# Second and last product of an attention, MoE, MoE kernel: T1's product goes ahead of T2's, and each sum is made in the step of its own product

## The chip, the cores and the metric

The kernel runs on one core of one Trainium2 chip. The metric is device time of one launch in microseconds (us). Three runs of the kernel before gave 1398.18, 1399.5 and 1400.55, median 1399.5.

## The reference

The input goes through three parts. The first is an attention over 32 memory slots per head (8 batches, 8 heads, 576 positions, 64 wide); its output, taken as rows of 512, has 4608 of them. Then come two feed-forward blocks, one after the other, each with its own weights of 512 x 2048 and 2048 x 512:

```python
def _moe_ref(x, w_in, w_out):          # x is 4608 x 512
    h = x @ w_in
    r = np.maximum(h, 0.0)
    g = r * r
    return (g @ w_out).astype(np.float32)

def _moe2_ref(x, w_in, w_out):
    h = x @ w_in
    g = h * (1.0 / (1.0 + np.exp(-h)))
    return (g @ w_out).astype(np.float32)

def reference(**kwargs):
    attn_out = _attn_ref(**attn_kwargs)
    x = np.ascontiguousarray(attn_out.transpose(0, 2, 1, 3)).reshape(B * S, H * D)
    x = _moe_ref(x=x, **moe_kwargs)
    return _moe2_ref(x=x, **moe2_kwargs)
```

## The kernel before

Four large products follow one another on TensorE (PE). The first (L635, first block of rows L612) joins the attention with `w_in` of the first feed-forward block. The **second product** is g1 times the first `w_out`, the third product (L940) is its result times the second `w_in`, and the **last product** is g2 times the second `w_out`. The second and the last are made by the same function, `second` (L735), with PE's matmuls on L821. The change touches these two alone.

The three later products use a scheme with seven products of half-size matrices in place of eight. The moving matrix of a block of 768 rows is cut in four quarters B11, B21, B12 and B22 (a quarter is half of the inner dimension by 384 rows, for all of that half's eight slices of 128). From them four sums are made: T1 = B12 - B11, T2 = B22 - T1, T3 = B22 - B12 and T4 = B21 - T2. The seven products take B11, B21, T2, T1, T3, B22 and T4 (`PRODUCTS`, L698), numbered n = 0 to 6, each with its own combination of the weights, which lies in slot n of the weight tiles W[q] (`slot`, L685; product 6 shares slot 1 with product 1, and `next_w`, L691, loads one in place of the other). There are eight weight tiles, q = 0 to 7, one for each pair of the inner dimension's slices.

Every factor is split in a part that the matmul takes exactly (`hi`, made by a cast on ScalarE, ACT, L792) and the rest (`lo`, a subtraction on VectorE, DVE, L793); the text calls them cast and split. Three matmuls of 128 x 128 by 384 columns stand for one product of such pairs.

**Steps.** `second` runs over `(b, n, h)`: six blocks b of 768 rows, seven products n, four quarters h of the inner dimension (two slices each). One step has 12 matmuls of 384 columns: 2 slices, 2 halves of the output, 3 pairings. The step's moving tile c has six buffers, and `combos` (L770), which makes the sums, the cast and the split for one step, is called four steps ahead of the step's matmuls (`AHEAD`, `ahead`). The sums are made in place: T1 over B11 (L780), T3 over B12 (L786), T4 over B21 (L789); T2 has a tile of its own (L784). Before the change T1's sum and T2's are both made in the steps of T2, T3's in the steps of T1, T4's in the steps of T3. In the second product the quarters are squared on ACT first (L768), B11 and B21 in the steps of n = 0, B12 and B22 in those of n = 1.

**Tiles of the quarters.** The next block's quarters are loaded (L760, `r<-g`, 16 transfers per block) into tiles that the block before frees (`FREED`, L730): B11 into the tile of B11 (which held T1), B21 into the tile of T2, B12 and B22 into their own, and the new T2 goes where T4 was. For block 0 the function `begin` orders the loads of quarters and weights: `begin_out1` for the second product, `begin_out2` for the last one.

**Results.** PSUM has three kinds of banks, a, b and c. B11's product starts bank a, T2's, T3's and T4's add to it; B21's is in b; T1's starts c and B22's adds to it. `evict` (L702) runs after each product: after n = 0 ACT copies a to u1 (L707); after n = 1 DVE adds b to u1, which is C11 (L705), and it is sent to memory out of u1; after n = 2 ACT copies a to u2 (L712); after n = 3 ACT copies c to u3 (L714); after n = 4 DVE adds a to u3 (C22); after n = 5 c to u2 (C12); after n = 6 ACT copies a (C21, L842). u1, u3 and C21's copy share one pair of buffers, u2 has a pair of its own. The transfers to memory are issued on L844.

**Order.** All DMAs named here are issued by SyncE (SP), in its order. The order of instructions in each engine's queue is fixed before the launch by a planner, which goes by the order of the program and by when it believes an instruction to be ready; it moves instructions far (sums ahead of splits, matmuls of one step between those of another). An engine takes its queue in that order.

Of the kernel before, what the change touches and what calls it, by code (L numbers as in the profile page):

```python
# [16 lines left out]
ALU = mybir.AluOpType  # L17
# [17 lines left out]
TB, TH = 6, 384  # L35
NQ = NF // 2
# [5 lines left out]
SLOTS = 6  # L42
# [35 lines left out]
def attention_moe_moe(ctx: ExitStack, tc, q, kv, phi, w_in1, w_out1, w_in2, w_out2, out):  # L78
# [42 lines left out]
    def hold(ins, until=10 ** 6, step=-1):  # L121

        if begun and len(begun) < until:
            after(ins, begun[step])
# [560 lines left out]
    def slot(n):  # L685
        return n if n < SLOTS else 1

    def load_w(src, q, n):
        return nc.sync.dma_start(W[q][:, slot(n)].bitcast(F32), src[q][:, n])

    def next_w(src, qs, n, last):  # L691

        if n == 1 or n == 6 and not last:
            for q in qs:
                load_w(src, q, 7 - n)
# [6 lines left out]
    def evict(n, t, s, c, copy3, done):  # L702
# [18 lines left out]
        else:  # L721
            done("C21", t["a"])

    QS = 2
    NH = NQ // QS
    HQ = NQ // 2
# [5 lines left out]
    def x_tile(i, shape, dtype, name):  # L732
        return (xa, xb, upool)[i // 4].tile(shape, dtype, tag=f"x{i}", bufs=1, name=name)

    def second(src, order, square, to, weights, begin, tiles=tuple(range(10))):  # L735

        raw = {}  # L740
        cc = {}
        places = [dict(zip(NAMES, range(5)))]
        for _ in range(1, TB):
            was = places[-1]
            places.append({name: was[of] for name, of in zip(NAMES, FREED)})

        def place_tiles(b, name):

            i = places[b][name]
            ts = [x_tile(tiles[2 * i + k], [P, HQ, TH], F32, "r") for k in range(2)]  # L750
            for h in range(NH):
                u = h * QS % HQ
                raw[b, name, h] = ts[h * QS // HQ][:, u:u + QS]
            return ts

        def quarters(b, names=("B11", "B21", "B12", "B22"), held=None):
            for name in names:
                for i, t in enumerate(place_tiles(b, name)):
                    for h in range(i * HQ, i * HQ + HQ, QS):
                        dma = nc.sync.dma_start(t[:, h - i * HQ:h - i * HQ + QS], src[b][:, order.index(name), h:h + QS])  # L760
                        if b == 1:
                            hold(dma, step=start)
                        if held:
                            held(dma)

        def squares(b, h, names):
            for name in names if square else ():
                nc.scalar.activation(raw[b, name, h], raw[b, name, h], AF.Square)  # L768

        def combos(b, n, h):  # L770

            tt = nc.vector.tensor_tensor
            name = PRODUCTS[n][0]
            r = lambda x: raw[b, x, h]
            if n == 0:
                squares(b, h, ("B11", "B21"))
            elif n == 1:
                squares(b, h, ("B12", "B22"))
            elif name == "T2":
                tt(r("B11"), r("B12"), r("B11"), op=ALU.subtract)  # L780
                raw[b, "T1", h] = r("B11")
                if h == 0:
                    place_tiles(b, "T2")
                tt(r("T2"), r("B22"), r("T1"), op=ALU.subtract)  # L784
            elif name == "T1":
                tt(r("B12"), r("B22"), r("B12"), op=ALU.subtract)  # L786
                raw[b, "T3", h] = r("B12")
            elif name == "T3":
                tt(r("B21"), r("B21"), r("T2"), op=ALU.subtract)  # L789
                raw[b, "T4", h] = r("B21")  # L790
            c = cc[b, n, h] = spool.tile([P, 2, QS, TH], F32R, tag="g", name="c")
            nc.scalar.copy(c[:, 0], r(name))  # L792
            tt(c[:, 1], r(name), c[:, 0].bitcast(F32), op=ALU.subtract)  # L793

        steps = [(b, n, h) for b in range(TB) for n in range(7) for h in range(NH)]

        def ahead(k):
            if k < len(steps):
                b, n, h = steps[k]
                if n == h == 0 and b:  # L800
                    quarters(b)
                combos(b, n, h)

        start = len(begun)
        begin(quarters)
        for k in range(AHEAD):
            ahead(k)
        for k, (b, n, h) in enumerate(steps):
            ahead(k + AHEAD)
            bank = PRODUCTS[n][1]  # L810
            if h == 0 and n == 0:
                ps = [{} for _ in range(2)]
                st = [{} for _ in range(2)]
            if h == 0 and n in FIRST:
                for o in range(2):
                    ps[o][bank] = psum.tile([P, TH], F32, tag=bank, bufs=4 if bank == "a" else 2, name=f"ps{bank}")
            x = cc.pop((b, n, h))
            for u in range(QS):
                for o in range(2):
                    for m, (wi, xi) in enumerate(((0, 0), (0, 1), (1, 0))):  # L820
                        mm = nc.tensor.matmul(  # L821
                            ps[o][bank], W[h * QS + u][:, slot(n), wi, o * P:(o + 1) * P], x[:, xi, u],
                            start=(n in FIRST and h == u == m == 0), stop=(h == NH - 1 and u == QS - 1 and m == 2),
                            skip_group_check=True,
                        )
                        if u == o == m == 0:
                            begun.append(mm)
            next_w(weights, range(h * QS, h * QS + QS), n, b == TB - 1)
            if h < NH - 1:
                continue  # L830
            for o in range(2):
                def tile_s(u, o=o):
                    if u not in st[o]:
                        st[o][u] = upool.tile([P, TH], F32, tag=UTAG[u], name=u)
                    return st[o][u]

                def done(c, bank, o=o, b=b):
                    if bank is None:
                        y = tile_s(SUM[c], o)
                    else:  # L840
                        y = upool.tile([P, TH], F32, tag="u1", name="y")
                        nc.scalar.copy(y, bank)  # L842
                    oh, half = int(c[1]) - 1, int(c[2]) - 1
                    nc.sync.dma_start(to(b, 2 * oh + o, half), y)  # L844
                evict(n, ps[o], tile_s, lambda c: tile_s(SUM[c]), nc.scalar.copy, done)
        return [tiles[2 * places[-1][name] + k] for name in FREED for k in range(2)]
# [6 lines left out]
    def begin_out1(quarters):  # L853

        last = len(begun) - 1
        n = 0

        def held(ins):
            nonlocal n
            hold(ins, step=min(last, last - EARLY + n * 3 // 4))  # L860
            n += 1

        for q in range(WR, WR + 2):
            for k in range(SLOTS):
                held(load_w(w1o, q, k))
        for k, name in enumerate(("B11", "B21", None)):
            for q in (*range(WR + 2, NQ), *range(WR)) if k == 1 else range(WR + 2, NQ):
                held(load_w(w1o, q, k))
            if name:
                quarters(0, (name,), held)  # L870
            if k == 1:
                quarters(0, ("B12", "B22"), held)
        for k in range(3, SLOTS):
            for q in range(WR + 2, NQ):
                held(load_w(w1o, q, k))

# [50 lines left out]
    for b in range(TB):  # L927
        for r in range(NQ // 2):
# [4 lines left out]
            for n, (_, bank) in enumerate(PRODUCTS):  # L933
# [12 lines left out]
                for q in qs:  # L946
# [5 lines left out]
                    def done(c, src, q=q):  # L952
                        if c == "C12":
                            nc.scalar.activation(gq[q][:, :3], gq[q][:, :3], AF.Silu)  # L954
                        elif c == "C21":
                            nc.scalar.activation(gq[q][:, 3], src, AF.Silu)
# [15 lines left out]

    def begin_out2(quarters):
        quarters(0, ("B11", "B21"))
        for q0, n0, n1 in ((0, 0, 4), (2, 0, 4), (4, 0, 2), (6, 0, 1), (6, 1, 2), (4, 2, 4), (6, 2, 3)):
            for n in range(n0, n1):
                for q in (q0, q0 + 1):
                    load_w(w2o, q, n)
            if q0 == 6 and n0 == 1:
                quarters(0, ("B12", "B22"))  # L980
        for n in range(3, SLOTS):
            for q in (range(NQ) if n > 3 else (6, 7)):
                load_w(w2o, q, n)

    second(g2, tuple(c.replace("C", "B") for c in order2), False,
# [46 lines left out]
```

## Time and profile before

| | |
|---|---|
| median of three runs | 1399.5 us |
| the profiled execution's own time | 1397.83 us |
| its span, first to last instruction | 1396.0 us |
| PE busy with matmuls | 1371.7 us (98%) |
| DVE busy | 965.6 us (69%) |
| ACT busy | 792.7 us (57%) |
| mean granted clock of PE | 0.997 |
| second product (L821) on PE | 327 to 684 us |
| last product (L821) on PE | 1029 to 1392 us |

All times in the views are from the span's start. A group's line has the engine, the operation, what it writes and reads, the count, the busy time, the mean duration of one in ns, and the idle time of the engine before it with what ended most of it. Matmuls overlap: one of 384 columns is listed with some 335 ns, while the next one starts well before that. PEclk is the clock that PE was granted, 1 being the full one. On the rows of a timeline, neighbours of one kind are merged with their count, and square brackets hold the engine's idle time before the row with what ended it.

### The profile page before, as it was taken

The numbers are of one execution on the slowest core, as the hardware profiler recorded it, in microseconds if no ns is written. First come the engines' busy times: TensorE is split into PE (matmuls) and PEld (weight loads), VectorE is DVE, ScalarE is ACT, GpSimd is POOL, SyncE is SP. The second block draws the span as 40 slices with busy tenths as digits, with TensorE's granted clock in tenths as the row PEclk, the third lists the DMA queues.
The fourth block names the chain that finished last, engine by engine and source line by source line (L and its number), as shares of the span: only waits on it lengthen the run. The fifth ranks groups of instructions, "written<-read, shape, count | busy, mean of one in ns | idle before, by whom it ended". The sixth has DMA issues, their size and how long they took to land.

```text
span 1396.0 us, 25396 instructions
## 1 busy us (share of the span) xinstructions
PE 1371.7 (98%) x9349; PEld 1312.6 (94%) x9349; DVE 965.6 (69%) x1578; ACT 792.7 (57%) x1305; POOL 22.6 (2%) x44
## 2 busy tenths in 40 slices
PE   7999999998999999999999999999998999999998
PEld 5778888888999999999999999999998999999998
DVE  5767676755798788979556756566448858768583
ACT  4656666666858678586355555555444444444442
POOL 0000000000000000000000000000000000000000
PEclk9999999999999999999999999999999999999999
DMA  9979998899778879789988788888998567564640
GB/s 329 361 273 344 333 345 304 278 327 370 260 247 307 274 238 344 243 294 322 359 299 289 268 297 276 283 279 285 369 399 319 160 226 234 190 230 154 227 155 35
DMA packets 208445, 388.25 MB, mean 278 GB/s; under 512 B 19264, under 2 KB 90944, under 8 KB 208320
## 3 DMA queue, kind: packets, MB, share of 16 engines
q1 hardware_dynamic: 208320, 386.62, 80.1%
q8 instruction: 74, 1.21, 0.3%
q14 instruction: 51, 0.42, 0.1%
HBM read 253.38 MB, written 133.17 MB: 277 GB/s over the span
## 4 chain that ended last, share of the span: by engine, by line
PE 87%; DMA 8%; DVE 3%; SPq 1%; issue 1%; ACT 1%; POOL 0%; ACTq 0%; DVEq 0%; POOLq 0%
PE psa L821 28%; PE psc L821 14%; PE psa L940 14%; PE h L635 10%; PE psc L940 7%; PE psb L821 7%; PE psb L940 4%; DMA g<-gt 2%; PE pswp L443 2%; DMA kv<-kv 2%; DMA r<-g 1%; DMA st<-moe_w_in 1%; PE pskv L400 1%; DMA ws<-w1o 1%; PE pssc L443 0%
## 5 line engine op out<-in xcount | busy, mean ns | idle before, releaser
L793 DVE TENSOR_TENSOR c<-r,c 128x768 fp32r<-128x768 f32 x336 | 316.6, 955 | 159.1 <-ACT c L792 158.8
L821 PE MATMUL psa<-c,ws 128*128 128x384 f32 x2304 | 414.5, 337 | 5.8 <-DVE c L793 3.5
L821 PEld LDWEIGHTS psa<-c,ws 128*128 128x128 f32 x2304 | 404.7, 189 | 7.3 <-DVE c L793 4.5
L792 ACT CAST c<-r 128x768 fp32r<-128x768 f32 x336 | 278.9, 836 | 229.0 <-PE psa L821 120.1
L940 PE MATMUL psa<-xc,ws 128*128 128x384 f32 x1152 | 217.3, 336 | 0.0
L635 PEld LDWEIGHTS h<-at,wp 128*128 128x128 f32 x1344 | 180.5, 188 | 30.6 <-ACT gt L644 15.8
L821 PE MATMUL psc<-c,ws 128*128 128x384 f32 x1152 | 205.7, 335 | 2.8 <-ACT c L792 2.8
L821 PEld LDWEIGHTS psc<-c,ws 128*128 128x128 f32 x1152 | 201.0, 188 | 3.1 <-ACT c L792 3.1
L940 PEld LDWEIGHTS psa<-xc,ws 128*128 128x128 f32 x1152 | 202.3, 188 | 0.0
L635 PE MATMUL h<-at,wp 128*128 128x288 f32 x1344 | 195.7, 300 | 1.7 <-ACT gt L644 1.7
L940 PE MATMUL psc<-xc,ws 128*128 128x384 f32 x576 | 110.9, 335 | 0.0
L821 PE MATMUL psb<-c,ws 128*128 128x384 f32 x576 | 104.2, 336 | 0.0
L940 PEld LDWEIGHTS psc<-xc,ws 128*128 128x128 f32 x576 | 101.2, 188 | 0.0
L821 PEld LDWEIGHTS psb<-c,ws 128*128 128x128 f32 x576 | 100.8, 188 | 0.0
L644 ACT ACTIVATE gt<-h 128x576 f32<-128x576 f32 x112 | 72.2, 649 | 45.8 <-PE h L635 40.9
L768 ACT ACTIVATE r<-r 128x768 f32<-128x768 f32 x96 | 79.2, 846 | 17.5 <-DMA r<-g 17.2
L205 DVE TENSOR_TENSOR pp<-pw,pp 128x256 f32<-128x256 f32 x148 | 60.5, 419 | 34.8 <-ACT pp L204 33.0
L204 ACT CAST pp<-pw 128x256 fp32r<-128x256 f32 x148 | 58.0, 404 | 30.2 <-PE psa L940 14.7
L954 ACT ACTIVATE g2t<-g2t 128x1152 f32<-128x1152 f32 x48 | 54.8, 1164 | 30.0 <-DVE g2t L705 29.9
L162 ACT CAST top<-st 128x256 f16<-128x256 bf16 (+1 forms) x112 | 57.9, 527 | 21.5 <-PE psa L940 12.0
L707 ACT COPY u<-psa 128x384 f32<-128x384 f32 x72 | 34.2, 476 | 57.1 <-DVE g2t L705 20.9
L166 DVE SCALAR_TENSOR_TENSOR pw<-st,top 128x256 int32<-128x256 int32 x96 | 41.1, 432 | 32.6 <-ACT top L162 31.2
(101 smaller groups left out, 1179.5 us busy)
## 6 DMA issues: line engine op xcount, KB each, us to landing
r<-g SPq DMA_DIRECT2D x192, 384.0 KB, 5.6
g<-g2t SPq DMA_DIRECT2D x48, 768.0 KB, 6.9
ws<-w2i SPq DMA_DIRECT2D x136, 256.0 KB, 5.2
ws<-w2o SPq DMA_DIRECT2D x136, 256.0 KB, 3.9
ws<-w1o SPq DMA_DIRECT2D x116, 256.0 KB, 4.2
g<-gt SPq DMA_DIRECT2D x64, 384.0 KB, 5.7
kv<-kv SPq DMA_DIRECT2D x32, 516.0 KB, 6.7
st<-moe_w_out SPq DMA_DIRECT2D x64, 256.0 KB, 4.9
```

The lines of the kernel that those rows point to most:

```text
L162: ins = nc.scalar.copy(top.bitcast(F16).rearrange("p (n h) -> p n h", h=2)[:, :, 1], flat.bitcast(BF16).rearrange("p (n h) -> p n h", h=4) ...
L166: to_f32.last = nc.vector.scalar_tensor_tensor(f.bitcast(I32), flat.rearrange("p (n w) -> p n w", w=2)[:, :n, 1], 13, top, op0=ALU.logical ...
L204: held(nc.scalar.copy(hi, w[:, of]))
L205: tt(lo, w[:, of], hi.bitcast(F32), op=ALU.subtract)
L635: mm = nc.tensor.matmul(h[:, half, :HALF], wp[b, j][:, g, s, fo:fo + P], attnT[b][:, x, g, tk], start=(k == 0), stop=(k == len(ops) - 1),)
L644: nc.scalar.activation(gt[:, f % 2].rearrange("p (h t) -> p h t", h=2), h[:, :, :HALF], AF.Relu)
L768: nc.scalar.activation(raw[b, name, h], raw[b, name, h], AF.Square)
L792: nc.scalar.copy(c[:, 0], r(name))
L793: tt(c[:, 1], r(name), c[:, 0].bitcast(F32), op=ALU.subtract)
L821: mm = nc.tensor.matmul(ps[o][bank], W[h * QS + u][:, slot(n), wi, o * P:(o + 1) * P], x[:, xi, u], start=(n in FIRST and h == u == m == 0 ...
L940: mm = nc.tensor.matmul(ps[q][bank], W[q][:, slot(n), wi, k * P:(k + 1) * P], x[:, xi, k], start=(n in FIRST and k == 0 and m == 0), stop= ...
L954: nc.scalar.activation(gq[q][:, :3], gq[q][:, :3], AF.Silu)
```

## The change

The steps are taken in the order B11, B21, T1, T2, T3, B22, T4 (`ORDER`); the products keep their numbers, slots and evictions. T1's sum is made in T1's steps, T2's in T2's, T3's in T3's (each ahead of the cast), and T4's in the steps of B22, behind that step's split. In `begin_out1` and `begin_out2` the loads of slot 3 (T1) go ahead of those of slot 2 (T2) where these two differ.

```diff
+    ORDER = (0, 1, 3, 2, 4, 5, 6)
     QS = 2
...
-            elif name == "T2":
+            elif name == "T1":
                 tt(r("B11"), r("B12"), r("B11"), op=ALU.subtract)
                 raw[b, "T1", h] = r("B11")
+            elif name == "T2":
                 if h == 0:
                     place_tiles(b, "T2")
                 tt(r("T2"), r("B22"), r("T1"), op=ALU.subtract)
-            elif name == "T1":
+            elif name == "T3":
                 tt(r("B12"), r("B22"), r("B12"), op=ALU.subtract)
                 raw[b, "T3", h] = r("B12")
-            elif name == "T3":
-                tt(r("B21"), r("B21"), r("T2"), op=ALU.subtract)
-                raw[b, "T4", h] = r("B21")
             c = cc[b, n, h] = spool.tile([P, 2, QS, TH], F32R, tag="g", name="c")
             nc.scalar.copy(c[:, 0], r(name))
             tt(c[:, 1], r(name), c[:, 0].bitcast(F32), op=ALU.subtract)
-
-        steps = [(b, n, h) for b in range(TB) for n in range(7) for h in range(NH)]
+            if name == "B22":
+                tt(r("B21"), r("B21"), r("T2"), op=ALU.subtract)
+                raw[b, "T4", h] = r("B21")
+
+        steps = [(b, n, h) for b in range(TB) for n in ORDER for h in range(NH)]
...
-        for k, name in enumerate(("B11", "B21", None)):
+        for k, name in ((0, "B11"), (1, "B21"), (3, None)):
...
-        for k in range(3, SLOTS):
+        for k in (2, 4, 5):
             for q in range(WR + 2, NQ):
                 held(load_w(w1o, q, k))
...
-        for q0, n0, n1 in ((0, 0, 4), (2, 0, 4), (4, 0, 2), (6, 0, 1), (6, 1, 2), (4, 2, 4), (6, 2, 3)):
+        for q0, n0, n1 in ((0, 0, 4), (2, 0, 4), (4, 0, 2), (6, 0, 1), (6, 1, 2), (4, 2, 4), (6, 3, 4)):
...
-        for n in range(3, SLOTS):
-            for q in (range(NQ) if n > 3 else (6, 7)):
+        for n in (2, 4, 5):
+            for q in (range(NQ) if n > 2 else (6, 7)):
                 load_w(w2o, q, n)
```

## Rows read from the trace of the kernel before

**Rows 1.** Page, the chain that ended last: share of the span by engine.
```profile
PE 87%; DMA 8%; DVE 3%; SPq 1%; issue 1%; ACT 1%; POOL 0%; ACTq 0%; DVEq 0%; POOLq 0%
```

**Rows 2.** Groups by line: busy, mean ns of one, idle before and its releasers.
```profile
L821 PE MATMUL psa<-c,ws 128*128 128x384 f32 x2304 | 414.5, 337 | 5.8 <-DVE c L793 3.5 <-ACT c L792 2.2
L940 PE MATMUL psa<-xc,ws 128*128 128x384 f32 x1152 | 217.3, 336 | 0.0
...
L821 PE MATMUL psc<-c,ws 128*128 128x384 f32 x1152 | 205.7, 335 | 2.8 <-ACT c L792 2.8
...
L821 PE MATMUL psb<-c,ws 128*128 128x384 f32 x576 | 104.2, 336 | 0.0
```

**Rows 3.** Timeline of PE, second product: start us, us, instruction, count, [idle before].
```profile
344.67 2.60 PE L821 MATMUL psa<-c,ws 128*128 128x384 f32 x14
350.05 0.62 PE L821 MATMUL psc<-c,ws 128*128 128x384 f32 x2 [2.77 <-ACT c L792]
351.01 7.75 PE L821 MATMUL psa<-c,ws 128*128 128x384 f32 x34 [0.34 <-DVE c L793]
358.59 8.16 PE L821 MATMUL psc<-c,ws 128*128 128x384 f32 x46
366.59 8.52 PE L821 MATMUL psa<-c,ws 128*128 128x384 f32 x48
...
525.82 4.35 PE L821 MATMUL psa<-c,ws 128*128 128x384 f32 x24
```

**Rows 4.** Timeline of PE, last product.
```profile
1044.37 6.08 PE L821 MATMUL psb<-c,ws 128*128 128x384 f32 x34
1051.25 0.61 PE L821 MATMUL psa<-c,ws 128*128 128x384 f32 x2 [0.79 <-ACT c L792]
1054.65 3.76 PE L821 MATMUL psa<-c,ws 128*128 128x384 f32 x12 [2.79 <-DVE c L793]
...
1066.63 8.16 PE L821 MATMUL psc<-c,ws 128*128 128x384 f32 x46
...
1133.15 8.52 PE L821 MATMUL psa<-c,ws 128*128 128x384 f32 x48
```

**Rows 5.** Timeline of DVE, second product, blocks 0 and 3.
```profile
334.15 1.83 DVE L780 TENSOR_TENSOR r<-r 128x768 f32<-128x768 f32 x2
337.77 1.83 DVE L780 TENSOR_TENSOR r<-r 128x768 f32<-128x768 f32 x2 [1.79 <-ACT r L768]
...
528.99 2.69 DVE L793 TENSOR_TENSOR c<-r,c 128x768 fp32r<-128x768 f32 x3
```

**Rows 6.** Stretches: length, busy us of PE, PEld, DVE, ACT, POOL; PEclk, DMA, GB/s.
```profile
351.00:354.00 3.00, 2.99 (x10) 3.00 (x11) 3.00 (x4) 0.47 (x1) 0.00 (x0) 0.53 0.65 204
...
1055.00:1058.00 3.00, 3.00 (x11) 3.00 (x11) 3.00 (x5) 0.83 (x1) 0.00 (x0) 0.54 1.05 402
```

**Rows 7.** Timeline of DVE, last product, blocks 0 and 1.
```profile
1044.92 0.95 DVE L780 TENSOR_TENSOR r<-r 128x768 f32<-128x768 f32 x1
...
1046.70 2.69 DVE L780 TENSOR_TENSOR r<-r 128x768 f32<-128x768 f32 x3
...
1053.65 0.95 DVE L793 TENSOR_TENSOR c<-r,c 128x768 fp32r<-128x768 f32 x1
...
1126.23 0.96 DVE L793 TENSOR_TENSOR c<-r,c 128x768 fp32r<-128x768 f32 x1 [1.50 <-ACT c L792]
```

**Rows 8.** Timeline of ACT, last product, blocks 0 and 1.
```profile
1050.36 0.83 ACT L792 CAST c<-r 128x768 fp32r<-128x768 f32 x1 [4.58 <-DVE r L784]
...
1124.46 1.00 ACT L712 COPY u<-psa 128x384 f32<-128x384 f32 x2 [0.72 <-PE psa L821]
```

**Rows 9.** The eight loads of quarters issued from 1030 to 1044 us, by tile: time to landing.
```profile
DMA to landing us min/median/max: 6.6/7.8/8.6
```

**Rows 10.** Timeline of SP, last product, block 1: C11 sent out.
```profile
1119.33 0.87 SPq L844 DMA_DIRECT2D out<-u  x2
```

**Rows 11.** The same two transfers by tile: time from issue to landing.
```profile
DMA to landing us min/median/max: 6.7/6.7/6.7
```

## The prediction

> **What bounds the kernel now.** I read the page first, then the order of time on PE around its gaps, and then the same stretches on DVE, ACT and SP. The chain that ended last runs on PE for 87% of the span [rows 1]: time is won only where PE stands still or runs at the lower clock. The costliest groups say how much that is. The product between the two that change (L940) has no idle time before its matmuls at all, and the 4032 matmuls of L821, in both products that change, have 5.8 + 2.8 = 8.6 us [rows 2].
>
> The order of time on PE places 6.69 of the 8.6 us: block 0 of each product, where PE comes out of B21 and meets T2. In the second product it waits 2.77 and 0.34 us for T2's and T1's casts and splits [rows 3], in the last one 0.79 and 2.79 us [rows 4]. The other 1.9 us lie before the first step of the second product, which the change leaves alone. So blocks 1 to 5 run without a gap already, and the change can only cost there. Block 0 is the one whose B12 and B22 are loaded while PE is already at B11 and B21, so that all sums of the block are squeezed between that load and PE's coming. In later blocks the splits run ahead of PE, though not far everywhere: in block 3 of the second product T2's third split starts 528.99 and ends 0.95 us later [rows 5], when PE is just through T2's first 24 matmuls (525.82, 4.35 us) [rows 3]. No stall, and 0.2 us of lead.
>
> A wait costs more than its length. After the gaps the granted clock is 0.53 and 0.54 [rows 6], the lower level of 1.2 GHz; at the full one 46 matmuls start in the 8.00 us from 358.59 to 366.59, 0.174 us each [rows 3]. So I count by starts. Second product: from 344.67 to 358.59 there are 14 + 2 + 34 = 50 matmuls in 13.92 us; at full pitch 8.70; lost 5.22 us [rows 3]. Last product: from 1044.37 to 1066.63 there are 96, 34 in the first row shown and 62 in the seven rows up to the last one, in 22.26 us; at full pitch 16.70; lost 5.56 us [rows 4]. Together 10.78 us: 6.69 of waits and 4.09 of lower clock, some 2.0 us per place. That is all the change can win.
>
> **The change, part by part.** *T1's product ahead of T2's.* T1 = B12 - B11 needs no B22 and one sum; T2 needs B22, T1 and a second sum. Last product: T1's first sum starts 1044.92 and takes 0.95 [rows 7], so it is there at 1045.87. ACT stands idle until 1050.36, waiting 4.58 us for T2's sum [rows 8]; a cast of 0.83 would end at 1046.7. T1's split then takes the next place on DVE: 1046.70 if it goes ahead of the other three T1 sums, 1049.31 behind them; it ends at 1047.7 or 1050.3. PE is through what it has of B21 at 1050.3 (1044.37 + 34 x 0.174) [rows 4]. Now T2's first split starts 1053.65, and five sums of T2, T3 and T4 stand between T1's sums and it [rows 7]. I take the later place: a wait of 0, and 0.5 us if one more operation of 0.87 (three sums in 2.69 us) goes in front. T1's other splits need one place in each step of 2.09 us, in which DVE has 2.4.
>
> Second product: T1's first two sums start 334.15 and take 1.83, the other two end at 339.6 [rows 5]; PE comes to the product after B21 at 344.67 [rows 3]. That is over 5 us for a cast and a split: 0. T2 is now due 8.36 us later, at 353.0. The most that DVE can put in front of T2's first split is T1's four splits, four sums each of T2, T3 and T4, C11's two adds (1 us) and the split itself: 17 x 0.87 + 1.0 = 15.8 us from 339.6, to 355.4, a wait of 2.4 us; the least is none. I take none, as T1's splits and T2's pair come first in the program. For the two places together I leave 1.0 us.
>
> *Fewer sums per step.* The number of sums, casts and splits stays (four sums and seven splits for each h and block). The peak of three operations per step, in T2, becomes two. Outside block 0 nothing waits, so this is worth 0; at the most it adds 4 x 0.87 = 3.5 us of lead in block 3, where the T4 sums can move behind T2's splits.
>
> *T4's sum after B22's split.* It frees T2's tile later, into which SP loads the next block's B21. At the latest the fourth T4 sum ends 5 x 8.36 + 6.3 - 8.1 + 0.95 = 41 us into a block of 58.5 (B22's last step, less the lead that splits have below); its load takes at most 8.6 us [rows 9], and eight loads of B12 and B22 queue behind it on SP, which took no more than 14 us for eight in its fullest stretch [rows 9]: 64. PE asks for T1 of the next block at 58.5 + 8 x 2.09 = 75. Hidden by 11 us, taken as 0. With that cover gone, every us late comes back at five block borders in each product.
>
> *Copy of u3 one product earlier.* u3 shares its two buffers with u1, which leaves as C11. The copy (L714) moves to the place where L712 copies u2 now, and gains a wait for C11's transfer. Block 1 of the last product: issued from 1119.33 on in 0.87 us [rows 10], landed 6.7 us after each issue [rows 11], the second by 1126.5; the copy at that place starts 1124.46 [rows 8]. ACT would stand up to 2.0 us, with the casts of T3 and B22 queued behind it, and behind these their splits and PE. Their lead: T3's second split ends 1126.23 + 0.96 = 1127.19 [rows 7] and is used at 1133.15 + 2.09 = 1135.24 [rows 4], 8.05 us. Price 0; without that cover 2.0 us per block.
>
> The Trainium skill (DMA: Bandwidth & Descriptors, section "Anatomy of one DMA — SWDGE (gpsimd) path") has a fixed 2.0 us per transfer plus its bytes at 436 GB/s, fitted on GpSimd's path. An estimate from it for C11's 128 x 384 words is 2.45 us, a landing at 1122.3, and no wait for the copy at all. The row here says 6.7 us on SP's queue, so the added wait stands; the sum would be the same by both, and by the page rival D falls.
>
> *Weights.* Slot 3 of the last quarters loads ahead of slot 2; the count of loads stays. T1's last step needs it 6.3 us (three steps) after T1 begins, as T2's needed slot 2 before: 0. Bounds 0 and 1.7 us, one place in that queue at 14 us for eight.
>
> **Sum.** 10.78 - 1.0 = 9.78 us off the profiled execution, 1397.83 (span 1396.0 and 1.83 around it), to 1388.1. That execution lies 1.67 below the median shown, 1399.5; on that scale the forecast is 1389.7.
>
> **Rivals.**
> *A, forecast:* both stalls go, 1389.7; its own range 1388.5 to 1392.
> *B, one stays.* The last product's stall may be set by transfers more than by order: loads take up to 8.6 us there [rows 9], and T1's first split has 0 to 2.6 us of room. Against: the first T1 sum was done at 1045.87. 1399.5 - 5.22 = 1394.3; if the other one stays, 1399.5 - 5.56 = 1393.9.
> *C, the wait moves to T2.* DVE puts T3's and T4's sums ahead of T2's splits, as now, when 2.5 us passed between T2's cast (ended 1051.19) and its split. Waits of 2.4 and 2.5 us, and 2.0 us each at the lower clock, are 8.9; 10.78 - 8.9 = 1.9 is left: 1397.6. Against: T2 has 8.36 us more.
> *D, slower: the earlier copy of u3.* ACT waits for C11 in every block, and where casts have no lead PE waits too: 2.0 us, and 2.0 us of lower clock, 4.0 per place. It decides where the lead falls under 2 us, as in block 3 of the second product now. One such place takes 4.0 of the 9.78; four take 16, and 1399.5 - 9.78 + 16 = 1405.7. Against: 8.05 us of lead in the last product.
> *E, nothing.* The order in the queues is made by a planner, not by the program alone: two matmuls of T1 stand inside T2 already (350.05, x2) [rows 3]. It could go on serving T2 first. 1399.5.
>
> **Chances.** A 0.53, B 0.20, C 0.09, D 0.10, E 0.08. What a measurement here can tell from no change is about 0.2%, 2.8 us. A and B are faster, 0.73; C and E the same, 0.17; D slower, 0.10. The range leaves out D, half of E and what little lies below 1387.5: 1387.5 to 1399.8.
>
> **What would show it.** Right: PE's waits at L821 hold only the 1.9 us of the second product's first step; no stretch near a clock of 0.53 behind block 0's B21; psc follows psb on PE; ACT's wait of 4.58 us for L784 is gone; L714 waits for a transfer by up to 2 us with PE unmoved. Wrong: PE waits for c at T1 or T2 in block 0 (B, C), or in blocks 1 to 5 just after L714 waited for a transfer (D); psa of T2 still straight behind psb (E).

## The result: slower by 0.55%

The changed kernel takes 1406.81 us (median of 7 runs) against 1399.5 before (7 runs): a ratio of 1.0055, 95% interval 1.0041 to 1.0069. The forecast, 1389.7, had the wrong sign, and the time lies outside the range. The profiled execution took 1406.94 us (span 1405.2, mean granted clock 0.998). In this kernel's lines the two products' matmuls are L823, the middle product's L942, the cast L791, the split L792, the square L769; the copies to u1, u2 and u3 stay L707, L712 and L714.

The groups of the page that answer to [rows 2]:

```profile
L823 PE MATMUL psa<-c,ws 128*128 128x384 f32 x2304 | 411.2, 336 | 2.4 <-ACT c L791 1.5 <-ACT u L712 0.5 <-DVE c L792 0.4
L942 PE MATMUL psa<-xc,ws 128*128 128x384 f32 x1152 | 217.9, 336 | 1.3 <-ACT u L707 1.3
L823 PE MATMUL psc<-c,ws 128*128 128x384 f32 x1152 | 213.1, 339 | 10.2 <-ACT c L791 7.9 <-ACT u L714 1.3 <-DVE c L792 1.0
```

Bank a's idle time fell from 5.8 to 2.4 us; the forecast left 1.9, and the other 0.5 is a new wait for the copy L712. Bank c's rose from 2.8 to 10.2, and 7.9 of it waits for casts. The order of time on PE says where; the rows are block 0 of the second product, its block 2, and block 0 of the last product:

```profile
345.69 6.79 PE L823 MATMUL psc<-c,ws 128*128 128x384 f32 x38
352.31 0.52 PE L823 MATMUL psa<-c,ws 128*128 128x384 f32 x2
352.67 1.90 PE L823 MATMUL psc<-c,ws 128*128 128x384 f32 x10
354.41 8.16 PE L823 MATMUL psa<-c,ws 128*128 128x384 f32 x46
...
473.76 7.99 PE L823 MATMUL psa<-c,ws 128*128 128x384 f32 x45
484.18 0.75 PE L823 MATMUL psc<-c,ws 128*128 128x384 f32 x2 [2.43 <-ACT c L791]
485.17 3.26 PE L823 MATMUL psc<-c,ws 128*128 128x384 f32 x10 [0.24 <-DVE c L792]
488.27 8.55 PE L823 MATMUL psa<-c,ws 128*128 128x384 f32 x48
...
1077.81 12.76 PE L823 MATMUL psa<-c,ws 128*128 128x384 f32 x70
1091.87 8.34 PE L823 MATMUL psc<-c,ws 128*128 128x384 f32 x46 [1.30 <-ACT u L714]
```

In block 0 psc (T1) follows psb (B21) with no gap, where [rows 3] had 2.77 us. In block 2 PE ends T2 (psa), does B22's first quarter (psc x2 and x10), which belongs behind T3, and then T3 (psa x48 at 488.27); it stands before that quarter for 2.43 us. Counted by starts, 45 + 2 + 10 = 57 matmuls take 14.51 us from 473.76 to 488.27; at 0.174 each they need 9.92, so 4.6 us are lost. Blocks 1 to 4 of the second product all have this place and lose some 1.7, 4.6, 3.0 and 5.1 us, 14.4 together; 9.4 of it are waits, the rest is mostly lower clock behind them. In block 0 ScalarE copies T2's result as T2 ends. In block 5 the planner fills the place with 12 matmuls of the middle product, and PE doesn't wait there. The middle product loses 1.5 at its head (the wait for L707 above).

What was won: block 0 of the second product lost 5.22 us and now 0.2; that of the last product 5.56 and now 2.1 (the wait of 1.30 for L714 is in it). So 8.5 us won, 15.9 paid, 7.4 net. The two profiled executions differ by 9.1; 1.0 of the rest is a later start of the second product (328.22 against 327.21), where nothing was changed, and 0.7 isn't placed.

### The profile page after: what moved, and what is told of

It reads as the page before. It is cut to its first block, busy times and chain, and to the rows that moved or that the text cites. A ratio compares the mean times of both kernels' runs of the same rounds, so it can differ in the third digit from the quotient of the medians.

```text
span 1405.2 us, 25352 instructions
## 1 busy us (share of the span) xinstructions
PE 1374.6 (98%) x9349; PEld 1312.3 (93%) x9349; DVE 965.6 (69%) x1578; ACT 792.9 (56%) x1305; POOL 22.6 (2%) x44
## 4 chain that ended last, share of the span: by engine, by line
PE 85%; DMA 6%; DVE 5%; ACT 3%; issue 1%; SPq 1%; POOL 0%; ACTq 0%; DVEq 0%; POOLq 0%
PE psa L823 25%; PE psa L942 14%; PE psc L823 13%; PE h L635 11%; PE psc L942 7%; PE psb L823 6%; PE psb L942 3%; DMA r<-g 2%; PE pswp L443 2%; PE pskv L400 1%; PE h L612 1%; DVE c L792 1%; DMA w2i<-pp 1%; DMA g<-gt 1%; DMA kv<-kv 1%
## 5 line engine op out<-in xcount | busy, mean ns | idle before, releaser
L792 DVE TENSOR_TENSOR c<-r,c 128x768 fp32r<-128x768 f32 x336 | 316.0, 953 | 156.3 <-ACT c L791 153.5
L823 PE MATMUL psa<-c,ws 128*128 128x384 f32 x2304 | 411.2, 336 | 2.4 <-ACT c L791 1.5
L791 ACT CAST c<-r 128x768 fp32r<-128x768 f32 x336 | 279.0, 836 | 235.5 <-PE psa L823 113.9
L823 PEld LDWEIGHTS psa<-c,ws 128*128 128x128 f32 x2304 | 402.7, 188 | 4.2 <-ACT c L791 1.7
L823 PE MATMUL psc<-c,ws 128*128 128x384 f32 x1152 | 213.1, 339 | 10.2 <-ACT c L791 7.9
L942 PE MATMUL psa<-xc,ws 128*128 128x384 f32 x1152 | 217.9, 336 | 1.3 <-ACT u L707 1.3
L823 PEld LDWEIGHTS psc<-c,ws 128*128 128x128 f32 x1152 | 203.0, 190 | 12.9 <-ACT c L791 9.2
L942 PEld LDWEIGHTS psa<-xc,ws 128*128 128x128 f32 x1152 | 202.2, 188 | 1.6 <-ACT u L707 1.6
L942 PE MATMUL psc<-xc,ws 128*128 128x384 f32 x576 | 110.9, 335 | 0.0
L823 PE MATMUL psb<-c,ws 128*128 128x384 f32 x576 | 104.5, 336 | 0.0
L942 PEld LDWEIGHTS psc<-xc,ws 128*128 128x128 f32 x576 | 101.2, 188 | 0.0
L823 PEld LDWEIGHTS psb<-c,ws 128*128 128x128 f32 x576 | 100.8, 188 | 0.0
L769 ACT ACTIVATE r<-r 128x768 f32<-128x768 f32 x96 | 79.5, 845 | 21.2 <-DMA r<-g 20.9
L204 ACT CAST pp<-pw 128x256 fp32r<-128x256 f32 x148 | 57.8, 403 | 24.8 <-PE psa L942 11.8
L162 ACT CAST top<-st 128x256 f16<-128x256 bf16 (+1 forms) x112 | 57.7, 527 | 24.1 <-PE psa L942 12.9
L707 ACT COPY u<-psa 128x384 f32<-128x384 f32 x72 | 34.0, 475 | 54.5 <-DVE g2t L705 20.2
```

The lines of the kernel that those rows point to most:

```text
L162: ins = nc.scalar.copy(top.bitcast(F16).rearrange("p (n h) -> p n h", h=2)[:, :, 1], flat.bitcast(BF16).rearrange("p (n h) -> p n h", h=4) ...
L204: held(nc.scalar.copy(hi, w[:, of]))
L823: mm = nc.tensor.matmul(ps[o][bank], W[h * QS + u][:, slot(n), wi, o * P:(o + 1) * P], x[:, xi, u], start=(n in FIRST and h == u == m == 0 ...
L942: mm = nc.tensor.matmul(ps[q][bank], W[q][:, slot(n), wi, k * P:(k + 1) * P], x[:, xi, k], start=(n in FIRST and k == 0 and m == 0), stop= ...
```

## The experiments

The theory: T2's, T3's and T4's products all add to bank a. T2's result must be copied out (u2, L712) before T3's product may add to it. In the old order, a b a c a c a, a product on another bank always lies between two on bank a. The new one is a b c a a c a: T3 comes straight behind T2, and PE waits for ScalarE, either for the copy or for the cast of what the planner puts into the gap. The letters in the expectations are those of the experiments, not of the prediction's rivals.

**The new order in block 0 alone.**
```diff
-    ORDER = (0, 1, 3, 2, 4, 5, 6)
+    FIRST_BLOCK = (0, 1, 3, 2, 4, 5, 6)
...
-        steps = [(b, n, h) for b in range(TB) for n in ORDER for h in range(NH)]
+        steps = [(b, n, h) for b in range(TB) for n in (range(7) if b else FIRST_BLOCK) for h in range(NH)]
```
(with the sums of blocks 1 to 5 in their old places)

> Block 0 of both products in the new order (T1 ahead of T2) with the new places of the sums; blocks 1 to 5 in the order and with the sums of before. Theory A (the adjacency: T2's and T3's products both add to bank a, and in the new order T3 comes straight behind T2, so that PE waits for ACT's copy of T2's result, or for what the planner pulls into the gap): blocks 1 to 4 of the second product lose nothing, block 0's gain of about 10 us stays in most part (block 0 of the second product may now pay for its own passage T2 to T3): 1388 to 1392 us, faster. Rival B (T4's sum made later frees a tile later, so that loads and ACT's squares come later): its late sum is gone from blocks 1 to 5, so this kernel comes out fast by B too; it is told apart by the next three. Rival C (u3's copy, made earlier, waits for C11's transfer): 1.6 us at most remain of it, at the last product's block 0: about 1390.

Measured: 1390.98 us, ratio to the kernel before 0.9931 (0.992 to 0.9943). In the second product PE waits only before its first step, as it did before the change. So nearly all that the new order gains lies in block 0, and what it costs in blocks 1 to 5; the one cost left in block 0 is the wait of 1.3 us for L714 in the last product. A second set of runs gave 1391.23, 0.9931 (0.9917 to 0.9945). This beats both kernels.

**The copy taken from another bank.**
```diff
-            nc.scalar.copy(s("u2"), t["a"])
+            nc.scalar.copy(s("u2"), t["b"] if copy3 == nc.scalar.copy else t["a"])
```

> The changed kernel, but in the second and last product ACT's copy behind T2's product reads bank b instead of bank a (so the values of C12 are other ones: that part of the computation is changed). T3's product then needs not wait for that copy; number and size of ACT's copies, the order of the products and the sums stay. Theory A: the stalls of blocks 1 to 4 of the second product (14.4 us) vanish, with the 1.6 us at the head of the middle product perhaps: 1389 to 1393 us. Rival B (T4's late sum) and rival C (u3's early copy): nothing of theirs is touched, so the time stays at 1405 to 1408 us. Rival D (ACT has too much to do there, whatever the banks): 1400 or more, with PE waiting for ACT's casts of T3 or B22.

Measured: 1390.51 us, 0.9931 (0.9918 to 0.9944). PE's waits in the second product, from 326 to 705 us (what waits, for what, us in total, times, longest):

```profile
PE psa L823 <- ACT c L791: 1.5, 1, 1.5
PE psa L823 <- DVE c L792: 0.4, 1, 0.4
```

Both lie before the product's first step. All of the 14.4 us are gone with as many products, sums and copies as before, and so is the wait of the middle product. The need to read bank a between T2 and T3 is therefore the cause. (C12's values are other ones in this kernel.)

**T4's sum moved back, and the sums moved without the order.**
```diff
             elif name == "T3":
                 tt(r("B12"), r("B22"), r("B12"), op=ALU.subtract)
                 raw[b, "T3", h] = r("B12")
+                tt(r("B21"), r("B21"), r("T2"), op=ALU.subtract)
+                raw[b, "T4", h] = r("B21")
...
-            if name == "B22":
-                tt(r("B21"), r("B21"), r("T2"), op=ALU.subtract)
-                raw[b, "T4", h] = r("B21")
```

> The changed kernel with T4's sum alone moved back, from the step of B22 to the step of T3 ahead of its cast, as before the change. Theory A: the stalls at the passage from T2 to T3 stay, 1404 to 1409 us. Rival B (the late sum of T4 frees its tile late, the next block's loads and squares are late, and ACT with them): the stalls go, 1389 to 1396 us. Rival C (u3's early copy): no change, about 1406 us.

```diff
-    ORDER = (0, 1, 3, 2, 4, 5, 6)
...
-        steps = [(b, n, h) for b in range(TB) for n in ORDER for h in range(NH)]
+        steps = [(b, n, h) for b in range(TB) for n in range(7) for h in range(NH)]
```
(T1's sum back in T2's step and the loads of weights in their old order; T3's and T4's sums stay where the change put them)

> The order of the products of before (T2, T1, T3), with T3's sum made in T3's step and T4's sum in B22's step behind its split: the moved sums without the new order. Theory A: T1's product lies between T2's and T3's again, so the blocks 1 to 4 have no stall at that passage; block 0 of both products still waits for T1 and T2 as before, a little less: 1396 to 1400 us. Rival B (late sum of T4): the stalls of 14.4 us appear in this order too, so 1405 to 1415 us.

Measured: 1409.29 us, 1.0057 (1.0044 to 1.0069) for the first; 1400.28, 1.0001 (0.9992 to 1.0009) for the second. With T4's sum back, PE still waits four times for a cast at the same passage:

```profile
PE psc L822 <- ACT c L793: 7.7, 4, 2.9
```

The late sum of T4 is not the cause, and moving T3's and T4's sums is worth nothing, as the prediction had it.

**The change in the last product alone.** (`for n in (range(7) if square else (0, 1, 3, 2, 4, 5, 6))`, with the sums to match.)

> The change made in the last product alone; the second product keeps the order and the sums of before. Theory A: the last product's gain stays (block 0 loses 2 us instead of 5.6), the second product is as before (6 us): 1394 to 1398 us, faster than before by 3 to 4 us. If the whole loss of the change belonged to both products alike, this kernel would lie halfway, 1402 to 1404 us.

Measured: 1395.38 us, 0.997 (0.9958 to 0.9981). The last product wins by the change; the whole loss belongs to the second product (the head of the middle product with it, which has no wait here). The main difference there is ScalarE's work: it squares the next block's quarters (L769), and it makes casts for later weights (L204, L162); the last product has neither.

**Without the squares.**
```diff
-    free = second(g1, ("B11", "B12", "B21", "B22"), True, lambda ...
+    free = second(g1, ("B11", "B12", "B21", "B22"), False, lambda ...
```

> The changed kernel with the squaring left out of the second product (that part of the computation is missing), so ScalarE has some 150 us less to do there, with the order of the products and of the sums the same. Theory A (adjacency, made dear by a full ScalarE queue): the second product becomes like the last one, where the same passage costs nothing: stalls of blocks 1 to 4 fall from 14 to 0 to 2 us, 1389 to 1394 us. Rival D (the copy's own latency behind T2's last matmul sets the stall, whatever else ScalarE does): 2 to 4 us a block stay, 1400 to 1407 us.

Measured: 1396.12 us, 0.9973 (0.9962 to 0.9984), above the range that theory A gave. (The squares are 79.5 us of ScalarE's busy time in the changed kernel, not the 150 of the expectation.) At the passage T2 to T3 one wait of four is left, and the middle product's head waits somewhat longer, with a lower clock behind it (3.6 us by starts):

```profile
PE psa L942 <- ACT u L707: 1.8, 1, 1.8
...
PE psc L823 <- DVE c L792: 0.9, 1, 0.9
```

The passage itself falls from 14.4 to 1.2 us. ScalarE's queue shows why. First the changed kernel, block 2 of the second product, where T2's last matmul starts at 473.76 + 44 x 0.174 = 481.4:

```profile
481.83 1.58 ACT L769 ACTIVATE r<-r 128x768 f32<-128x768 f32 x2
483.31 0.82 ACT L791 CAST c<-r 128x768 fp32r<-128x768 f32 x1
484.03 0.85 ACT L769 ACTIVATE r<-r 128x768 f32<-128x768 f32 x1
484.77 0.46 ACT L712 COPY u<-psa 128x384 f32<-128x384 f32 x1
485.13 0.85 ACT L769 ACTIVATE r<-r 128x768 f32<-128x768 f32 x1
485.88 0.47 ACT L712 COPY u<-psa 128x384 f32<-128x384 f32 x1
```

Then the kernel without squares, block 1:

```profile
420.68 1.00 ACT L712 COPY u<-psa 128x384 f32<-128x384 f32 x2 [0.67 <-PE psa L823]
```

With squares, ScalarE has a full queue when T2 ends: two squares, the cast that PE waits for, another square, then the copies, 3.4 us behind. Without them it stands idle, waiting for PE, and copies at once (in blocks 1, 2 and 4; in block 3 the copy follows a cast, and PE doesn't wait either).

The wait at the head of the middle product is not the squares' doing. In all six kernels whose planner put 12 or more of that product's matmuls into block 5 of the second product, its head waits 1.3 to 2.2 us for L707; in the other six it doesn't wait. No run tests that link by itself.

**The cast or the copy?** Two kernels ask whether the price is in what the planner pulled ahead (B22's first quarter, whose cast PE waits for) or in the copy itself. In one the cast is made on VectorE; in the other the quarter can't be pulled ahead.

```diff
-            nc.scalar.copy(c[:, 0], r(name))
+            (nc.vector.tensor_copy if n == 5 and h == 0 else nc.scalar.copy)(c[:, 0], r(name))
```

> The changed kernel with one thing moved: the cast of the first quarter of B22 (second and last product) is made on VectorE instead of ScalarE. PE waited 0.7 to 2.7 us for this cast on ScalarE at the passage from T2 to T3. Theory A1 (the price is that PE's written order pulls B22's first quarter into the gap, and its cast stands late in ScalarE's queue behind the next block's squares): the waits for the cast go, what stays is the wait for the copy of T2's sum, at most 0.5 us a block: 1392 to 1398 us. Theory A2 (the price is the copy of T2's result itself, which also stands behind squares in ScalarE's queue; what is pulled in ahead doesn't matter): the waits change their name from the cast to the copy and stay as long, 1402 to 1408 us.

```diff
-            nc.scalar.copy(c[:, 0], r(name))
+            cast = nc.scalar.copy(c[:, 0], r(name))
+            if square and (n, h) == (5, 0):
+                hold(cast)
...
```
(in the second product alone; written behind the first step of T3, and held until that step's first matmul)

> The changed kernel, with one more dependency in the second product: the cast of B22's first quarter waits until T3's first product has begun, so that it can't be put between T2 and T3. PE then goes straight from T2 to T3 and waits for the copy of T2's result alone. Theory A1 (the dear part is the quarter of B22 pulled ahead of its four steps of preparation; the copy alone is short): a wait of 0.5 to 1.5 us a block, named after the copy, 2.5 to 7.5 us in five blocks: 1394 to 1400 us. Theory A2 (the copy behind squares in ScalarE's queue is as late as the cast was): 2 to 3 us a block, 1402 to 1408 us.

Measured: 1406.68 us, 1.0051 (1.0038 to 1.0064), and 1407.04, 1.0052 (1.0033 to 1.0072). PE's waits in the second product with the cast on VectorE (the two on its first step left out):

```profile
PE psc L823 <- DVE c L792: 3.8, 4, 1.7
PE psc L823 <- DVE c L791: 2.6, 3, 1.0
PE psa L942 <- ACT u L707: 2.2, 1, 2.2
```

And with the quarter held, from 400 to 705 us:

```profile
PE psa L827 <- ACT u L712: 10.5, 4, 3.2
PE psa L948 <- ACT u L707: 1.5, 1, 1.5
```

Both times lie where A2 had them. With the cast elsewhere PE waits for VectorE's cast and split, not for the copy, as A2 had it, so this kernel alone doesn't decide. The other does, and A1 falls: with nothing pulled ahead PE goes from T2 to T3 and waits for the copy by name, 10.5 us in four blocks, and the total time is the same. The filler is about as late as the copy that it covers: in block 2 of the changed kernel it began at 484.18 and the first copy at 484.77.

**Another adjacency.**
```diff
-    ORDER = (0, 1, 3, 2, 4, 5, 6)
+    ORDER = (0, 1, 3, 2, 5, 4, 6)
```

> The changed order with T3 and B22 exchanged, in the second and last product: B11, B21, T1, T2, B22, T3, T4, so the banks are a b c a c a a: B22's product on bank c lies between T2 and T3, but T4 now comes straight behind T3 on bank a. What must be read from bank a between them is C22's sum, on VectorE, which has no squares in its queue. Theory A in the form that the queue of the reading engine makes the price: little or no stall at T3 to T4, and none at T2 to T3: 1389 to 1394 us. Theory A in the form that any two products in a row on one bank cost 2 to 4 us a block: the stalls move to the passage T3 to T4, 1402 to 1410 us.

Measured: 1404.57 us, 1.0034 (1.0022 to 1.0046). The waits moved to the passage from T3 to T4, with bank a on both sides of it:

```profile
PE psa L823 <- ACT c L791: 4.3, 4, 2.1
...
PE psa L823 <- DVE c L792: 1.9, 4, 0.5
```

One of each is the first step's 1.5 and 0.4; three of the casts waited for, 2.8 us, are at the new passage, where PE is given the next block's B11. So the stall follows the adjacency. It is smaller: by starts the new passage loses 0.9, 1.7, 1.1 and 4.7 us in blocks 0, 1, 2 and 4, 8.4 together, and nothing in block 3. That VectorE reads the bank there, and has no squares, doesn't help, though I had thought it would: the filler's cast is still on ScalarE. The last product stalls too (1.9 us).

**C11's transfer and the copy of u3.** In block 0 of the last product PE waits 1.30 us for L714. Here u3 doesn't share u1's buffers in block 0 (base: the new order in block 0 alone).
```diff
+    UTAG0 = {"u1": "u1", "u2": "u1", "u3": "u2"}
...
-                def tile_s(u, o=o):
+                def tile_s(u, o=o, tags=UTAG if b else UTAG0):
```

> The kernel with the new order in block 0 alone, and in block 0 of both products u3 takes the buffers of u2 and u2 those of u1. The copy to u3 then needs not wait for the transfer of C11 that left from u1's buffer. If that transfer is what holds the copy in the last product's block 0, the one wait of 1.3 us (1.6 us with what follows) there goes: 1388 to 1391 us, some 1.5 us below the same kernel without it. If the wait is for something else it stays and the time is the same within 0.5 us.

> The kernel with the new order in block 0 alone once more, beside the one with exchanged buffers on the same chip: 1390 to 1392 us; 1.5 us above the other if the transfer of C11 held the copy, equal to it if not.

Measured: 1395.11 us, 0.9961 (0.9948 to 0.9975), against 1391.23 for the kernel with shared buffers. The copy moved ahead, right behind T1, and PE no longer waits for it:

```profile
1058.38 1.00 ACT L715 COPY u<-psc 128x384 f32<-128x384 f32 x2 [1.04 <-PE psc L830]
```

So the tie to C11's buffer did set the copy's place. It did so through the planner's order, and not by the transfer's landing: in the changed kernel C11's two transfers were issued at 1080.9 and 1081.3 and landed 5.0 us later, and the copy followed only at 1091.34, straight behind a cast that had waited for PE:

```profile
1090.61 0.83 ACT L791 CAST c<-r 128x768 fp32r<-128x768 f32 x1 [1.25 <-PE psa L823]
1091.34 0.85 ACT L714 COPY u<-psc 128x384 f32<-128x384 f32 x2
```

With the exchanged buffers the other work came out in another order too, and B22's first quarter now waits for its split (the second product has 1.3 us of new waits besides):

```profile
PE psc L830 <- DVE c L799: 2.5, 1, 2.5
```

The forecast of 1.5 us less was wrong by the sign. How the planner came to this order isn't in the trace.

## Why the prediction was wrong

**The step that failed** is *T1's product ahead of T2's*. It was worked out for block 0, for the operands that PE waits for. For blocks 1 to 5 it was put at nothing: "So blocks 1 to 5 run without a gap already, and the change can only cost there", and the cost was then looked for at transfers only. What has to leave a bank was not priced. The prediction followed the copy that moves ahead (L714) and not the one whose place it takes: L712 moves to the border of T2 and T3, which both add to bank a. The runs show 14.4 us there, in blocks 1 to 4 of the second product, and 1.5 us at the middle product's head, in place of 0.

The rows of before had the price. PE passes from T2's bank a to T1's bank c in blocks 1 to 4 of the second product at:

```profile
417.13 3.65 PE L821 MATMUL psc<-c,ws 128*128 128x384 f32 x20
...
475.66 8.16 PE L821 MATMUL psc<-c,ws 128*128 128x384 f32 x46
...
534.18 3.12 PE L821 MATMUL psc<-c,ws 128*128 128x384 f32 x17
...
592.71 3.48 PE L821 MATMUL psc<-c,ws 128*128 128x384 f32 x19
```

and ScalarE copies T2's result at:

```profile
419.60 0.85 ACT L712 COPY u<-psa 128x384 f32<-128x384 f32 x2
...
479.21 0.84 ACT L712 COPY u<-psa 128x384 f32<-128x384 f32 x2
...
536.13 0.84 ACT L712 COPY u<-psa 128x384 f32<-128x384 f32 x2
...
595.32 0.84 ACT L712 COPY u<-psa 128x384 f32<-128x384 f32 x2
```

The copy starts 2.47, 3.55, 1.95 and 2.61 us after PE has left the bank, 10.6 us in four blocks, and T1's 8.4 us covered each. In every block of the last product it starts 0.3 us before PE goes on to T1, in block 1 at 1124.46 [rows 8]:

```profile
1124.79 8.52 PE L821 MATMUL psc<-c,ws 128*128 128x384 f32 x48
```

In blocks 0 and 5 of the second product it is the same, and none of these places has a stall in the changed kernel. The kernel with the quarter held waited 10.5 us in four blocks once the cover was gone. Block by block its waits (1.93, 3.17, 2.28 and 3.14) differ from the four above by up to 0.5, so that the sums meet so closely is luck. Taken from the forecast gain of 9.8, these rows alone give about no change; with lower clock after some waits, slower.

The Trainium skill (Perfetto Trace Analysis, section "Matmuls") says that independent groups of matmuls should rotate through different PSUM banks, so that the reading of one by ScalarE or VectorE overlaps the matmuls of the next. T2's and T3's products aren't independent, as T3 adds to what T2 left in the bank, so the sentence doesn't cover them as it stands; but the order of before had the overlap that it asks for, and I didn't weigh that the change gives it up. The trace shows the price of it: 14.4 us of stalls with two products in a row on bank a, none with the copy taken from bank b.

**The other steps.**
- *The gain in block 0*: right in kind. 8.5 of 10.78 us came back; I had 9.78. The 1.0 us allowed for both places is 2.3, and the larger part is the copy of u3.
- *Copy of u3*: right for blocks 1 to 4 of the last product, where ScalarE waited 1.6 to 2.3 us for C11's transfer and PE didn't; the lead of 8.05 us was read in block 1 and holds there. In block 0 "Price 0" is a wait of 1.30 us (1.9 by starts), and there it is the copy's place in ScalarE's queue that made it late. C11's transfers landed 5.0 us after issue in that block, longer than the 2.45 us of the estimate.
- *T4's sum* and *fewer sums*: 0 and 0, as run.
- *Weights*: 0; no wait of PE at L823 names a DMA.
- *Rivals*: D has the sign and, with 1405.7, nearly the time, but not the mechanism. By it the stalls would stand behind a copy of u3 that waits for a transfer; they are gone when the copy of u2 reads another bank, with u3 as it was. So D's nearly right time is luck, and its 0.10 was not for what happened.

## What to carry to other kernels

When products change places, write their banks down in the new order. Where one bank stands twice in a row, the next product waits for the reader of the first. The price is in the trace before the change: how long after PE leaves a bank does its copy start, in every stage and not only in the one the change is for. Here that lag told the four places with a stall from the others, in one kernel and with hindsight. An engine with slack on average (ScalarE is busy 57% of the span) can still be 3 us late at the one place where someone begins to wait for it, and a planner's filler, prepared by the same engine, is as late.

## What the runs showed of the hardware

I charged 2.0 us of lower clock to each wait. The granted clock doesn't follow a wait's length. The columns are the stretch, its length, the busy time of PE, PEld, DVE, ACT and POOL, PEclk, DMA share and GB/s. With B22's quarter held, behind a wait of 1.93 us and behind one of 3.17:

```profile
422.00:425.00 3.00, 2.79 (x10) 2.80 (x11) 2.73 (x7) 3.00 (x6) 0.00 (x0) 0.63 1.05 389
486.00:489.00 3.00, 3.00 (x18) 3.00 (x18) 1.28 (x2) 3.00 (x6) 0.00 (x0) 1.00 0.94 370
```

The shorter wait was followed by the lower level (1.2 GHz) for most of three microseconds, the longer one by the full 2.4 GHz. In the changed kernel two of the four passages of the second product were followed by the lower level. Nor is it a property of the kernel: the kernel with the new order in block 0 alone was profiled twice, on two chips, and its second product began with the same waits, 1.46 us and 0.38. In the first execution the full clock followed, in the second the lower one:

```profile
330.00:333.00 3.00, 3.00 (x19) 3.00 (x18) 3.00 (x4) 2.26 (x4) 0.00 (x0) 1.00 1.05 361
330.00:333.00 3.00, 3.00 (x11) 3.00 (x11) 3.00 (x4) 2.20 (x4) 0.00 (x0) 0.54 1.05 412
```

The same 46 matmuls behind these waits took 8.26 and 9.82 us, so two profiled executions can differ by 1.6 us at one wait with the kernel unchanged. What decides the clock stays open.
